# Attention and routed experts on one core: first expert's scaling spread, six matmuls of zeros first, last 128 tokens in two halves

## The chip, the cores and the metric

One core of a Trainium2 chip. The time is the device time of one execution in microseconds (us). A core has TensorE (PE, matmuls; PEld is its weight load), VectorE (DVE), ScalarE (ACT), GpSimd (POOL) and SyncE (SP, which here only issues DMAs). They run their own instruction streams in order and wait for each other by semaphores.

## What is computed

```python
# attention: 8 batches, 8 heads, 576 positions, 64 per head, 128 features
proj = x @ w_phi;  proj = proj - max(abs(proj))        # for q and for k
phi  = concat(exp(proj), exp(-proj))
kv, z = phi(k).T @ v, sum(phi(k))
attn = (phi(q) @ kv) / (phi(q) @ z + 1e-6)
# experts: x = attn as 4608 tokens of 512, 8 experts of 512 -> 1024 -> 512
P = exp(x @ w_gate - max)                               # 4608 x 8
for _ in range(8):                                      # rows, then columns
    P /= P.sum(1) + 1e-9;  P /= P.sum(0) + 1e-9;  P *= N / E
out = sum(P[:, e] * (relu(x @ w1[e]) @ w2[e]) for e in range(8))
```

Every token goes through every expert; P only weighs their outputs.

## The kernel before, in words

**Stages.** Attention runs first, pair of heads by pair of heads. Its results are turned and kept as `xT` (features on partitions, 4608 tokens in nine groups of 512, bf16). While attention still runs, and while the table P is normalised in eight rounds, TensorE already computes the first expert (`up0` and `down0`), unweighted, into one f32 accumulator `acc[g]` (128 x 4 x 512) for each of the nine groups. When P is there, each `acc[g]` is scaled by P's first column, and experts 1 to 7 are added to it. So 36 scalings (4 for each group; line 1240) stand between the first expert and the second.

**Experts 1 to 7.** The work of one expert on one group is a unit. Both matrix products of a unit are done with seven products of half-size blocks instead of eight. The first (`up7`) runs as 14 small products of four matmuls of 128x128 by 128x256 each; the second (`down7`) as 7 products of eight. All of them are recorded at line 1078 (`product`). In `up7` several products go into the same PSUM bank one after the other, and ScalarE copies the state of the bank to a buffer U in between (line 1106), so the next product into that bank waits for the copy. VectorE adds U to another bank and writes the hidden activations `hT` (line 1110); ScalarE writes others with a relu (line 1115). In `down7` ScalarE weighs a bank with P into V (line 1230) and GpSimd adds V to `acc` (line 1233), or VectorE does it in one step (line 1218). The products of `down7` of one group are mixed with those of `up7` of the next (`ORDER`); the first unit, group 0 of expert 1, has no such partner.

**Order.** Nothing is issued as it is written. Each operation is recorded with an engine, an estimated duration, and lists of keys that it reads and writes (`Plan.op`). `Plan.schedule` then picks again and again the operation that can start first by those estimates, an earlier record winning a tie, and so fixes the order on each engine. ScalarE's estimate is el/1200 + 0.09 us, which gives a scaling of 512 elements 0.52 us. The keys shape only this order; the waits on the chip come from what each instruction really reads and writes.

**Beginning.** SP, ACT and POOL issue loads of q, k, v and w_phi. TensorE first turns blocks of k and q (line 545, transposes with `identf`), VectorE casts w_phi (line 820) and the turned block (line 549), TensorE computes scores (line 468, recorded in the helper `mm`), and ScalarE takes exponentials (line 464).

**End.** The last unit (expert 7, group 7) computes its second product in the plain way (`down8`): four blocks of 128 tokens (`ts` = 2, 3, 0, 1), eight matmuls of 512 columns each (line 468), one VectorE step that weighs with P and adds to `acc` (line 1167), and one store of 256 KB (line 956).

Of the kernel before, what the change touches and what calls it, by code (L numbers as in the profile page):

```python
# [12 lines left out]
ALU = mybir.AluOpType  # L13
# [215 lines left out]
def kernel(  # L229
# [11 lines left out]
    nc = tc.nc  # L241
# [49 lines left out]
    def pe(cols, fn, r=(), w=(), takes=()):  # L291
        plan.op("PE", max(cols / 2400.0 + 0.0025, 0.032), 0.32, fn, r, w, takes)
# [10 lines left out]
    def dma(queue, nbytes, rate, fn, r=(), w=()):  # L303

        plan.op(queue, 0.8 if queue == "POOL" else 0.6, 0.0, fn, r, w, (), nbytes / rate / (125 / 100))
# [45 lines left out]
    def new(tag):  # L351
        return banks.new(int(tag[1])) if tag in ("P1", "P2") else R[tag].new()
# [29 lines left out]
    def load_qk(b, hh, nh, t, r=()):  # L382

        o = hh % 4
        keys = [o // 2] if nh == 2 else [0, 1]
        if b < 2:
            g = t["f"]
            for x, src in ((1, k), (0, q)):
                i = 2 * x + o // 2
                dma("SP", nh << 17, 268, lambda x=x, src=src, i=i: nc.sync.dma_start(  # L390
                    out=acc[g][:, i:i + nh // 2].rearrange("p a (h c) -> p (a h) c", h=2),
                    in_=src[b, hh:hh + nh, 0:SM].rearrange("h (p j) d -> p h (j d)", j=NJ)),
                    r, [("acc", g, 2 * x + n) for n in keys])
            return
        for x, src in ((1, k), (0, q)):
            dma("POOL", nh << 17, 200, lambda x=x, src=src: nc.gpsimd.dma_start(
                out=t["qk"]()[:, x, o:o + nh],
                in_=src[b, hh:hh + nh, 0:SM].rearrange("h (p j) d -> p h (j d)", j=NJ)),
                r, [(t["qk"], x, i) for i in keys])
# [67 lines left out]
    def mm(out_, lhsT, rhs, start, stop):  # L467
        nc.tensor.matmul(out_, lhsT=lhsT, rhs=rhs, start=start, stop=stop)  # L468
# [310 lines left out]
    def akey(g):  # L779
        return ["late"] * (g >= NA) + ["P"] * (g >= 9)  # L780
# [27 lines left out]
    for b in range(2):  # L808
        for i in range(2):
            halves[b, i] = new_half(b, i)  # L810
    load_qk(0, 0, 2, halves[0, 0])
    for i, (queue, eng) in enumerate((("ACT", nc.scalar), ("POOL", nc.gpsimd))):
        dma(queue, 1 << 15, 100, lambda i=i, eng=eng: eng.dma_start(
            out=wphi_f[64 * i:64 * i + 64, :], in_=w_phi), w=[f"wphi_f{i}"])
# [136 lines left out]
        expert0(i)  # L951


    def store(g, ts, one=0):
        if one:
            dma('SP', 1 << 18, 320, lambda: nc.sync.dma_start(
                out=out[g * S:g * S + SM].rearrange('(p j) d -> p j d', j=NJ)[:, ts:ts + 1],
                in_=acc[g][:, ts:ts + 1, :]),
                [('acc', g, ts, j) for j in range(2)], [('out', g, ts)])
        elif g < 8:  # L960
            if ts % 2:
                dma("SP", 1 << 19, 320, lambda: nc.sync.dma_start(
                    out=out[g * S:g * S + SM].rearrange("(p j) d -> p j d", j=NJ)
                    [:, ts - 1:ts + 1], in_=acc[g][:, ts - 1:ts + 1, :]),
                    [("acc", g, t, j) for t in (ts - 1, ts) for j in range(2)], [("out", g, ts)])
        else:
            for i in range(2):
                b = 2 * ts + i
                rows = slice(i * 64, i * 64 + 64)
                dma("SP", 1 << 17, 320, lambda b=b, rows=rows: nc.sync.dma_start(  # L970
                    out=out[b * S + SM:(b + 1) * S], in_=acc[8][rows, ts, :]),
                    [("acc", 8, ts, j) for j in range(2)], [("out", 8, b)])
# [184 lines left out]
    def down8(e, g, hT, w2):  # L1157

        for ts in (2, 3, 0, 1):
            py = new("P1")  # L1160
            for fc in range(8):
                i, j = fc // 4, ts // 2
                pe(512, lambda py=py, ts=ts, fc=fc: mm(
                    py(), hT[fc // 4]()[:, fc % 4, ts * 128:ts * 128 + 128], w2()[:, fc, :],
                    fc == 0, fc == 7), [(hT[i], fp, j) for i in range(2) for fp in range(2)]
                    + [(w2, i, j) for i in range(2) for j in range(2)] + ["P"], [py])
            dve(580, lambda py=py, ts=ts: nc.vector.scalar_tensor_tensor(
                out=acc[g][:, ts, :], in0=py(), scalar=P[:, 4 * g + ts, e:e + 1],
                in1=acc[g][:, ts, :], op0=ALU.mult, op1=ALU.add),
                [py, "P"], [("acc", g, ts, j) for j in range(2)])  # L1170
            store(g, ts, 1)

    def down7(e, g, hT, B7):

# [63 lines left out]
        if e == 1 and g < 9:  # L1238
            for ts in range(4):
                act(512, lambda ts=ts: nc.scalar.activation(  # L1240
                    out=acc[g][:, ts, :], in_=acc[g][:, ts, :], func=ACT.Copy, bias=0.0,
                    scale=P[:, 4 * g + ts, 0:1]), ["P", ("acc", g, ts)] + akey(g),
                    [("acc", g, ts, j) for j in range(2)])
        x, y, z = new("P1"), new("P1"), new("P1")

# [90 lines left out]
```

## Time and profile before

| | us |
|---|---|
| runs, median of 3 (lowest, highest) | 1036.96 (1035.57, 1037.59) |
| the profiled execution | 1036.16 |
| its span, first to last instruction | 1034.4 |
| PE busy, share of the span | 98% |
| ScalarE busy, share of the span | 69% |

The stages in the span: attention and the first expert up to 253 us, experts 1 to 7 from there to 1023 us, the plain second product and the last store from 1023 us to the end.

A row of a group or of the timeline names line, engine, operation, output<-inputs and shape; in brackets stand the engine's idle time before it and what ended it. Line numbers are those of the kernel before.

### The profile page before, as it was taken

To read this page: it belongs to the slowest core of one execution; us is meant where nothing else is said; L and a number is where in the kernel's file an instruction comes from. 1 tells how busy PE (TensorE), PEld (TensorE's weight loads), DVE (VectorE), ACT (ScalarE), POOL (GpSimd) and SP (SyncE) were. 2 spreads that over 40 slices of the span, in tenths; PEclk is the share of its full clock that TensorE was granted. 3 is DMA by queue.
4 is the path that set the end of the run, shared out by engine and by line. 5 is a ranking of instruction groups with operands and counts; after the bars stand their busy time and mean duration, and the time that the engine had idled before them with its cause. 6 is when DMAs were issued, how large, how long until landed. Compare 5 with 4: busy or idle time off the path is not lost.

```text
span 1034.4 us, 24481 instructions
## 1 busy us (share of the span) xinstructions
PE 1013.8 (98%) x9476; PEld 843.0 (81%) x9512; DVE 823.7 (80%) x1626; ACT 710.9 (69%) x1569; POOL 462.8 (45%) x534
## 2 busy tenths in 40 slices
PE   7899999999999999999999999999999999999998
PEld 5666666645788888888888888888888888888886
DVE  7999998987677788778777787788677877786775
ACT  7999999837966666666666656666666566666653
POOL 5877675400243443434443444434444433334442
PEclk9999999999999999999999999999999999999999
DMA  9998996085311161115211341134111611114333
GB/s 261 175 172 145 174 162 103 2 206 140 83 42 52 46 120 41 42 46 100 73 44 50 82 83 42 42 83 92 33 52 44 131 43 42 42 51 124 123 123 123
DMA packets 105237, 93.93 MB, mean 91 GB/s; under 512 B 45392, under 2 KB 80272, under 8 KB 105120
## 3 DMA queue, kind: packets, MB, share of 16 engines
q1 hardware_dynamic: 71360, 68.44, 24.3%
q0 software_dynamic: 33680, 23.90, 16.5%
q8 instruction: 74, 1.21, 0.5%
q14 instruction: 43, 0.35, 0.1%
q10 hardware_dynamic: 80, 0.03, 0.0%
HBM read 94.98 MB, written 14.16 MB: 106 GB/s over the span
## 4 chain that ended last, share of the span: by engine, by line
PE 92%; ACT 4%; DVE 3%; issue 1%; DMA 0%; DVEq 0%; POOLq 0%
PE P L1078 73%; PE P L468 17%; ACT acc L1240 2%; PE P L667 1%; DVE m L460 1%; ACT k L464 1%; PE P L706 1%; ACT q L464 0%; DMA wphi_f<-in_w_phi_dram 0%; DVE xb L687 0%; ACT U L1106 0%; DVE P L679 0%; PE P L672 0%; DVE S L986 0%; DVE m_r L460 0%
## 5 line engine op out<-in xcount | busy, mean ns | idle before, releaser
L1233 POOL TENSOR_TENSOR acc<-acc,V 128x512 f32<-128x512 f32 x248 | 316.1, 1281 | 440.5 <-ACT V L1230 437.6
L1110 DVE CUSTOM_DVE_ANT_0 hT<-P,U 128x512 bf16<-128x512 f32 x378 | 255.1, 687 | 105.9 <-ACT U L1106 56.7
L1106 ACT COPY U<-P 128x512 f32<-128x512 f32 x378 | 217.9, 590 | 139.0 <-PE P L1078 131.0
L1230 ACT ACTIVATE V<-P 128x256 f32<-128x256 f32 x496 | 205.6, 474 | 124.4 <-PE P L1078 119.2
L1218 DVE SCALAR_TENSOR_TENSOR acc<-P,acc 128x256 f32<-128x256 f32 x372 | 160.0, 478 | 73.7 <-PE P L1078 71.6
L1078 PEld LDWEIGHTS <-w 128*128 128x128 bf16 x2016 | 197.2, 98 | 25.2 <-issue 2.0
L1078 PEld LDWEIGHTS <-S 128*128 128x128 bf16 x1984 | 194.2, 98 | 22.4
L1078 PEld LDWEIGHTS <-T 128*128 128x128 bf16 x1512 | 147.9, 98 | 19.7 <-issue 2.5
L1078 PEld LDWEIGHTS <-hT 128*128 128x128 bf16 x1488 | 145.5, 98 | 17.1 <-DVE hT L1110 0.3
L1078 PE MATMUL P<-X,w 128*128 128x256 bf16 x1008 | 154.9, 273 | 0.4 <-ACT U L1106 0.4
L1078 PE MATMUL P<-xT,w 128*128 128x256 bf16 x1008 | 152.5, 273 | 0.9 <-ACT acc L795 0.5
L1078 PE MATMUL P<-X,T 128*128 128x256 bf16 x1008 | 148.6, 273 | 1.5 <-ACT U L1106 1.5
L1078 PE MATMUL P<-w,hT 128*128 128x256 bf16 x992 | 143.4, 273 | 0.0
L1078 PE MATMUL P<-T,S 128*128 128x256 bf16 x1056 | 136.3, 273 | 0.0
L1078 PE MATMUL P<-w,S 128*128 128x256 bf16 x928 | 126.5, 273 | 0.0
L460 DVE TENSOR_REDUCE m<-P 128x4 f32<-128x512 f32 x128 | 83.7, 679 | 3.4 <-PE P L468 2.1
L593 POOL TENSOR_TENSOR v<-v_m,em 128x512 bf16<-128x512 f32 x64 | 67.0, 1046 | 43.1 <-ACT em L464 39.0
L986 DVE TENSOR_TENSOR S<-hT 128x1024 bf16<-128x1024 bf16 x124 | 83.4, 709 | 0.3 <-ACT hT L1115 0.3
L1115 ACT ACTIVATE hT<-P 128x512 bf16<-128x512 f32 x126 | 74.2, 604 | 12.4 <-PE P L1078 11.9
L468 PE MATMUL P<-w,hT 128*128 128x512 bf16 x303 | 77.1, 379 | 0.9 <-DVE m L460 0.2
L1078 PE MATMUL P<-xT,T 128*128 128x256 bf16 x504 | 76.0, 273 | 0.3
L468 PE MATMUL P<-xT,w 128*128 128x512 bf16 x271 | 71.4, 379 | 1.0 <-ACT q L464 0.3
(95 smaller groups left out, 1096.5 us busy)
## 6 DMA issues: line engine op xcount, KB each, us to landing
X<-xd SPq DMA_DIRECT2D x126, 256.0 KB, 2.6
w<-in_moe_w_dram POOLq DMA_DIRECT2D x14, 1024.0 KB, 10.1
v_m<-in_v_dram SPq DMA_DIRECT2D x14, 512.0 KB, 5.2
out_dram<-acc SPq DMA_DIRECT2D x14, 512.0 KB, 2.7
xd<-S SPq DMA_DIRECT2D x18, 256.0 KB, 2.4
qk<-in_k_dram POOLq DMA_DIRECT2D x12, 256.0 KB, 5.5
qk<-in_q_dram POOLq DMA_DIRECT2D x12, 256.0 KB, 6.5
w<-in_moe_w_dram POOLq DMA_DIRECT2D x8, 256.0 KB, 7.7
```

The lines of the kernel that those rows point to most:

```text
L460: dve(el, lambda: nc.vector.tensor_reduce(out=dst(), in_=src(), axis=AX.X, op=ALU.max, apply_absolute_value=True), r, w)
L468: nc.tensor.matmul(out_, lhsT=lhsT, rhs=rhs, start=start, stop=stop)
L593: pool(512, lambda y=y, em=em: nc.gpsimd.tensor_tensor(out=s["v"][y]()[:, :, 0:D], in0=t["v"]()[:, h0:h0 + 2].rearrange("p a (b c) -> p (a ...
L986: lambda: f.tensor_tensor(out=out_(), in0=x(), in1=y(), op=op), r, w, **kw)
L1078: pe(256, lambda i=i, k=k, z=z: nc.tensor.matmul(bank()[:, 256 * i:256 * i + 256], lhsT=lhs(k, i), rhs=rhs(k), start=first and z, stop=k = ...
L1106: act(512, lambda: nc.scalar.copy(out=u[fp][n]().rearrange("p a b -> p (a b)"), in_=x[fp]()), [x[fp]], [u[fp][n]])
L1110: dve(500, lambda: nc.vector._custom_dve(ADD_SAT, out=out_(fp, i, j), in0=bank[fp]().rearrange("p (a b) -> p a b", a=2), in1=u[fp][n](), s ...
L1115: act(512, lambda: nc.scalar.activation(out=out_(fp, i, j), in_=x[fp]().rearrange("p (a b) -> p a b", a=2), func=ACT.Relu, bias=0.0, scale ...
L1218: dve(330, lambda n=n, ts=ts: nc.vector.scalar_tensor_tensor(out=acc[g][:, ts, 256 * j:256 * j + 256], in0=bank()[:, 256 * n:256 * n + 256 ...
L1230: act(390, lambda n=n: nc.scalar.activation(out=u()[:, n, :], in_=bank()[:, 256 * n:256 * n + 256], func=ACT.Copy, bias=0.0, scale=P[:, 4 ...
L1233: pool(670, lambda: nc.gpsimd.tensor_tensor(out=acc[g][:, 2 * i:2 * i + 2, 256 * j:256 * j + 256], in0=acc[g][:, 2 * i:2 * i + 2, 256 * j: ...
L1240: act(512, lambda ts=ts: nc.scalar.activation(out=acc[g][:, ts, :], in_=acc[g][:, ts, :], func=ACT.Copy, bias=0.0, scale=P[:, 4 * g + ts, ...
```

## The change

Three edits. A memset of zeros in the first 512 columns of `xT` and six matmuls on them stand ahead of all other work of TensorE; `xT` is written over later by its real contents. The last block of tokens (`ts` = 1 in `down8`) is computed, added and stored as two halves of 256 columns. The scaling of group g gets one more key to read, (`acc`, g-2, 0, 0), whose last writer is an addition to group g-2 by expert 1; so the planner places it after that.

```diff
@@ at the start
     load_qk(0, 0, 2, halves[0, 0])
+    dve(128, lambda: nc.vector.memset(xT[:, 0, 0:512], 0.0), w=[("xT", 0, 0)])
+    pz = new("P1")
+    for i in range(6):
+        pe(1024, lambda: mm(pz(), xT[:, 0, 0:128], xT[:, 0, 0:512], True, True),
+           [("xT", 0, 0)], [pz])
@@ def store
-    def store(g, ts, one=0):
-        if one:
-            dma('SP', 1 << 18, 320, lambda: nc.sync.dma_start(
-                out=out[g * S:g * S + SM].rearrange('(p j) d -> p j d', j=NJ)[:, ts:ts + 1],
-                in_=acc[g][:, ts:ts + 1, :]),
-                [('acc', g, ts, j) for j in range(2)], [('out', g, ts)])
+    def store(g, ts, js=()):
+        if len(js):
+            cols = slice(256 * js[0], 256 * js[-1] + 256)
+            dma("SP", len(js) << 17, 320, lambda: nc.sync.dma_start(
+                out=out[g * S:g * S + SM].rearrange("(p j) d -> p j d", j=NJ)[:, ts:ts + 1, cols],
+                in_=acc[g][:, ts:ts + 1, cols]),
+                [("acc", g, ts, j) for j in js], [("out", g, ts, j) for j in js])
@@ def down8
-            py = new("P1")
-            for fc in range(8):
...
-            store(g, ts, 1)
+            halves_ = 2 if ts == 1 else 1
+            n = DD // halves_
+            for c in range(halves_):
+                py, cols = new("P1"), slice(n * c, n * c + n)
+                for fc in range(8):
+                    i, j = fc // 4, ts // 2
+                    pe(n, lambda py=py, ts=ts, fc=fc, cols=cols, n=n: mm(
+                        py()[:, 0:n], hT[fc // 4]()[:, fc % 4, ts * 128:ts * 128 + 128],
+                        w2()[:, fc, cols], fc == 0, fc == 7),
...
+                js = range(2) if n == DD else (c,)
+                dve(580 * n // 512, lambda py=py, ts=ts, cols=cols, n=n:
+                    nc.vector.scalar_tensor_tensor(
+                        out=acc[g][:, ts, cols], in0=py()[:, 0:n],
+                        scalar=P[:, 4 * g + ts, e:e + 1], in1=acc[g][:, ts, cols],
+                        op0=ALU.mult, op1=ALU.add),
+                    [py, "P"], [("acc", g, ts, j) for j in js])
+                store(g, ts, js)
@@ def down7
                     out=acc[g][:, ts, :], in_=acc[g][:, ts, :], func=ACT.Copy, bias=0.0,
-                    scale=P[:, 4 * g + ts, 0:1]), ["P", ("acc", g, ts)] + akey(g),
+                    scale=P[:, 4 * g + ts, 0:1]), ["P", ("acc", g, ts)] + akey(g)
+                    + ([("acc", g - 2, 0, 0)] if g >= 2 else []),
                     [("acc", g, ts, j) for j in range(2)])
```

How the rows stand now. First ScalarE where the first expert ends and the second begins. `acc_78` to `acc_81` are the accumulators of groups 1 to 4, `acc_4252` that of group 5; L795 is the last eviction of the first expert, L1106 a copy to U. Before:

```order
L795 ACTIVATE acc_4254<-P 128x512
L1240 ACTIVATE acc_78<-acc_78,P 128x512 x3
L1240 ACTIVATE acc_79<-acc_79,P 128x512 x3
L795 ACTIVATE acc_4255<-P 128x512
L1240 ACTIVATE acc_79<-acc_79,P 128x512
L1240 ACTIVATE acc_80<-acc_80,P 128x512 x4
L1240 ACTIVATE acc_81<-acc_81,P 128x512
L795 ACTIVATE acc_4255<-P 128x512
L1106 COPY U<-P 128x512 x2
L1240 ACTIVATE acc_81<-acc_81,P 128x512
L1106 COPY U<-P 128x512
```

In the changed kernel, from the same eviction on (its lines are 1253 for the scaling, 1112 for the copy, 1121 for the relu, 1243 for V; accumulators 5 and up have other numbers):

```order
L795 ACTIVATE acc_4261<-P 128x512
L1253 ACTIVATE acc_78<-acc_78,P 128x512 x3
L795 ACTIVATE acc_4262<-P 128x512 x2
L1112 COPY U<-P 128x512 x6
L1121 ACTIVATE hT<-P 128x2x256 x2
L1243 ACTIVATE V<-P 128x256 x2
L1112 COPY U<-P 128x512
L1243 ACTIVATE V<-P 128x256 x2
L1112 COPY U<-P 128x512 x3
L1243 ACTIVATE V<-P 128x256 x2
L1253 ACTIVATE acc_79<-acc_79,P 128x512
```

The scalings of groups 0 and 1 keep their places; those of groups 2 to 8 (28 of 36) have moved behind the six copies, the two relus and the first V of group 0, and stand later one to three at a time among the copies of later units. The order of TensorE's products and of VectorE's sums changes with it from here on, the number of each does not.

Second, VectorE's and SP's first and last rows. VectorE's first rows, as a piece of the difference:

```order
-L818 MEMSET wphi_88 128x128
-L833 MEMSET vrd_89 128x520
...
+L812 MEMSET xT 128x256
+L823 MEMSET wphi_88 128x128
+L838 MEMSET vrd_89 128x520
```

One memset stands ahead of what was first there; TensorE's order begins with the six matmuls on `xT` and then has, up to the second expert, the same rows as before. VectorE's last rows, before:

```order
L1218 SCALAR_TENSOR_TENSOR acc_4253<-P,acc_4253 128x256 x2
L1110 ISA hT<-P,U 128x2x256
L1218 SCALAR_TENSOR_TENSOR acc_4253<-P,acc_4253 128x256 x2
L1167 SCALAR_TENSOR_TENSOR acc_4254<-P,acc_4254 128x512 x4
L1331 UNCONDITIONAL_BRANCH
```

And in the changed kernel:

```order
L1116 ISA hT<-P,U 128x2x256 x2
L1231 SCALAR_TENSOR_TENSOR acc_4260<-P,acc_4260 128x256 x4
L1179 SCALAR_TENSOR_TENSOR acc_4261<-P,acc_4261 128x512 x3
L1179 SCALAR_TENSOR_TENSOR acc_4261<-P,acc_4261 128x256 x2
L1345 UNCONDITIONAL_BRANCH
```

The fourth step of 512 columns has become two of 256; SP's last stores change in the same way, from four of 128x512 to three and two of 128x256.

More of the change, by code (lines that the diff above doesn't have):

```diff
@@ L1159, in down8 @@
         for ts in (2, 3, 0, 1):
-            py = new("P1")
-            for fc in range(8):
[L1162 to L1170, printed above, removed]
-            store(g, ts, 1)
+            halves_ = 2 if ts == 1 else 1
[7 more added lines that the diff above has]
+                        w2()[:, fc, cols], fc == 0, fc == 7),
+                        [(hT[i], fp, j) for i in range(2) for fp in range(2)]
+                        + [(w2, i, j) for i in range(2) for j in range(2)] + ["P"], [py])
+                js = range(2) if n == DD else (c,)
[6 more added lines that the diff above has]
+                store(g, ts, js)
     def down7(e, g, hT, B7):
```

## The prediction

> **What bounds the kernel now.** I read the page's header and its chain first, then the busy time by stretch, then the waits of the stretches where TensorE (PE) is not full.
>
> ```profile
> span 1034.4 us, 24481 instructions
> PE 1013.8 (98%) x9476; PEld 843.0 (81%) x9512; DVE 823.7 (80%) x1626; ACT 710.9 (69%) x1569; POOL 462.8 (45%) x534
> ...
> PE 92%; ACT 4%; DVE 3%; issue 1%; DMA 0%; DVEq 0%; POOLq 0%
> ```
>
> TensorE carries 92% of the chain; what is left to win is the 4% on ScalarE (ACT), the 3% on VectorE (DVE), and the end. Two tables by stretch (columns: stretch, its length, busy time and instruction count of each engine, clock, DMA share, GB/s), the second for the half-size matmuls of line 1078 alone, say where TensorE loses:
>
> ```profile
> 237.48:253.35 15.87, 15.78 (x74) 7.25 (x75) 12.74 (x29) 12.73 (x23) 0.75 (x1) 1.00 0.61 148
> 253.35:268.58 15.23, 12.23 (x98) 9.25 (x96) 9.93 (x16) 15.23 (x29) 0.89 (x1) 1.00 0.57 105
> 268.58:280.00 11.42, 11.42 (x105) 10.17 (x105) 7.87 (x15) 11.42 (x24) 5.08 (x4) 1.00 0.18 47
> ```
> ```profile
> 253.35:268.58 15.23, 11.75 (x94) 8.95 (x93) 1.00 0.57 105
> ...
> 280.00:1023.00 743.00, 742.92 (x6805) 665.54 (x6802) 1.00 0.26 67
> ```
>
> From 280 to 1023 us TensorE issues 6805 matmuls of 256 columns in 743.0 us, 109.2 ns each, without a gap: three quarters of the run cannot be touched by anything in this change. In 253.35 to 268.58 it issues only 93 (the 94th starts at the end) and some three of 512 columns, which at 109.2 and about 216 ns are worth 10.2 + 0.6 = 10.8 us. The stretch took 15.23, so **4.4 us are lost there**. ScalarE is the only engine that is busy in all of it (15.23 of 15.23), and the waits of TensorE and the chain of this stretch name it:
>
> ```profile
> PE P L1078 <- ACT U L1106: 1.9, 3, 1.3
> PE P L1078 <- ACT acc L795: 0.5, 1, 0.5
> PE P L1078 <- DVE hT L1110: 0.3, 1, 0.3
> ```
> ```profile
> by line: ACT acc L1240 61.1%; ACT U L1106 21.2%; issue 10.4%; ACT hT L1115 7.4%; ACT acc L795 3.2%; PE P L1078 1.8%
> ```
>
> The named waits come to 2.7 us; the rest of the 4.4 lies in the modelled ends of matmuls, which count a drained pipe as busy. Line 1240 is the scaling that the change touches.
>
> **Spreading the scaling: the large term.** The 36 scalings now stand together:
>
> ```profile
> L1240 ACT ACTIVATE acc<-acc,P 128x512 f32<-128x512 f32 x36 | 24.3, 754 | 1.1 <-DVE P L945 1.1
> ```
> ```profile
> 247.96 3.78 ACT L1240 ACTIVATE acc<-acc,P 128x512 f32<-128x512 f32 x6
> 251.63 0.59 ACT L795 ACTIVATE acc<-P 128x512 f32<-128x512 f32 x1
> 252.11 3.78 ACT L1240 ACTIVATE acc<-acc,P 128x512 f32<-128x512 f32 x6
> 255.79 0.59 ACT L795 ACTIVATE acc<-P 128x512 f32<-128x512 f32 x1
> 256.26 1.06 ACT L1106 COPY U<-P 128x512 f32<-128x512 f32 x2
> ```
> ```profile
> 254.10 0.49 PE L1078 MATMUL P<-xT,w 128*128 128x256 bf16 x3
> ...
> 267.48 0.60 PE L1078 MATMUL P<-X,T 128*128 128x256 bf16 x4 [1.33 <-ACT U L1106]
> ```
>
> A row of six takes 3.67 us from start to start, 0.61 each. The first product of the second expert is finished at 254.6 (254.10 + 0.49), but its copy to U, on which the next product into that bank waits, starts only at 256.26, 1.7 us late, behind a row of six. The changed order of ScalarE leaves the eight scalings of groups 0 and 1 where they were and then has all six copies of group 0, with the other 28 scalings one to three at a time in the units after it. The added entry in the planner's list of reads only orders the plan: no instruction waits for it on the chip, since a scaling reads acc of its own group and P. So ScalarE has nothing queued behind a new wait.
>
> Do 28 scalings fit later? One unit (one group of one expert) is 14 products of 4 and 7 of 8 matmuls, 112 x 109.2 ns = 12.2 us. ScalarE's share when no scaling is there, and what it bears with scalings:
>
> ```profile
> 280.00:400.00 120.00, 120.00 (x1102) 107.55 (x1100) 92.97 (x162) 75.14 (x159) 52.22 (x42) 1.00 0.27 63
> ```
>
> 75.14 of 120 is 63%, 7.7 us of a unit; four scalings add 4 x 0.61 = 2.4, which makes 83%. In 268.58 to 280 above it ran at 100%, scalings among its copies (the last of them at 278), while TensorE issued 105 matmuls in 11.42 us, 108.8 ns each. So single scalings between the copies cost TensorE nothing as long as no backlog stands before them. I therefore price the 28 moved scalings at zero; if that cover went, each would cost up to 0.61.
>
> What of the 4.4 us stays? Group 0 has no second products of an earlier group to fill TensorE, so some of its short waits may survive: I leave 0.7, about one copy and its handover (0.59 in the row of line 795, 0.53 a copy). VectorE, late next through its sums from U, has 9.93 of 15.23 us in use. Taken: **-3.7**; ends -4.6 (all of it, with 0.2 from the small gap before 253.35, where TensorE is busy 15.78 of 15.87) and -2.2 (half stays).
>
> **Zeros first: a small term.** The chain of the first microseconds, the matmul durations there, and the rows that bear on it:
>
> ```profile
> 1.26 3.86 DMA wphi_f<-in_w_phi_dram
> 5.40 0.70 DVE qkT L549
> 6.15 1.05 PE P L468 x4
> 7.22 2.06 ACT k L464 x4
> ```
> ```profile
> L468 PE MATMUL P<-wphi,qkT x6: 396/421/421, 6.1 to 7.2; 128*128 128x256 bf16 x6
> ```
> ```profile
> L545 PE MATMUL P<-identf,acc x8: 313/421/421, 8.7 to 10.2; 128*128 128x128 f32 x8
> ```
> ```profile
> L468 PE MATMUL P<-wphi,qkT x4: 272/272/273, 11.3 to 11.7; 128*128 128x256 bf16 x4
> ```
> ```profile
> 0.83 0.17 DVE L818 MEMSET wphi<- 128x128 uint32 x1 [0.83 <-PEq L1320]
> ...
> 3.58 2.13 PE L545 MATMUL P<-identf,acc 128*128 128x128 f32 x8 [3.58 <-DMA acc<-in_k_dram]
> 3.76 0.22 DVE L820 CAST wphi<-wphi_f 64x128 bf16<-64x128 f32 x1 [0.42 <-DMA wphi_f<-in_w_phi_dram]
> ...
> 17.89 1.09 PE L545 MATMUL P<-identf,acc 128*128 128x128 f32 x8 [0.52 <-DMA acc<-in_k_dram]
> ```
>
> The same matmul takes 421 ns at 6 us and 272 at 11 us: TensorE starts at half clock, and the one transpose of 313 ns among the eight from 8.7 to 10.2 puts the rise near 10.2 us (the clock column reads 1.00 throughout and does not show it). The memset doubles the width of the one that took 0.17, about 0.3 us, and VectorE's later work has 0.42 us of waiting before 3.76 to take it up. The zeros then run from about 1.2; a 512-column matmul at half clock is about 0.43 us, so six end near 3.8, and the first transposes start some 0.25 after their 3.58. That delay is free: the chain goes through the w_phi load (ending 5.1) and the cast at 5.40. The gain is that the four matmuls at 6.15 take 0.60, as at 11.3, instead of 1.05: -0.45, if the clock is up by then. ScalarE is busy without a break from 7.22 on, so this is all the chain can gain there; and at 17.89 TensorE already waits for a load, which does not come earlier, so part of it can be swallowed. Is the clock up by 6.15? The rise came 6.6 us after the first matmul at 3.58, but TensorE stood still for some 0.8 us of these; counted from 1.2 without that break it comes between 6 and 8 us, so it is about even whether the four profit. Taken: **-0.2**, about half of the gain, between -0.5 and +0.25 (no gain, and the transposes' delay on the path).
>
> The Trainium skill, "TensorE: Matmul & The Clock Gate", Part 1, has the clock rise after a free-running window of about 3.4 us that was busy, and Part 4 says that transposes do not count as busy in the same way. By that rule 2.6 us of zeros followed by transposes fill no window, and this term would be 0. This trace speaks against the second half: the clock rose while the eight transposes ran.
>
> **The last 128 tokens in two halves.** The end of the chain, the two shapes of VectorE's last step, and the stores:
>
> ```profile
> 1030.00 0.75 DVE L1167 SCALAR_TENSOR_TENSOR acc<-P,acc 128x512 f32<-128x512 f32 x1 [0.91 <-PE P L468]
> ```
> ```profile
> L1167 DVE SCALAR_TENSOR_TENSOR acc<-P,acc 128x512 f32<-128x512 f32 x4 | 3.0, 752 | 3.7 <-PE P L468 3.7
> L1218 DVE SCALAR_TENSOR_TENSOR acc<-P,acc 128x256 f32<-128x256 f32 x2 | 0.9, 475 | 0.0
> ```
> ```profile
> 1031.50:1032.00 0.50, 0.00 (x0) 0.00 (x0) 0.00 (x0) 0.00 (x0) 0.00 (x0) 1.00 0.77 291
> 1032.00:1032.50 0.50, 0.00 (x0) 0.00 (x0) 0.00 (x0) 0.00 (x0) 0.00 (x0) 1.00 0.63 234
> ```
> ```profile
> out_dram<-acc SPq DMA_DIRECT2D x8, 128.0 KB, 2.3
> out_dram<-acc SPq DMA_DIRECT2D x4, 256.0 KB, 2.4
> ```
>
> Sixteen matmuls of 256 columns replace eight of 512: 16 x 109.2 against 8 x 216 ns, no more than 0.02 us. The first half's step and store (0.33 us to issue) run beside the second half's 0.87 us of matmuls. After the last matmul stands a step of 0.475 instead of 0.752: -0.28. The last 256 KB move in about 0.85 us (the two rows: 291 and 234 GB/s for half a microsecond each, 262 KB), so half the bytes save up to 0.4 if rows of half the length move as fast; by the landings of 128 and 256 KB only 0.1, but those 128 KB stores come in pairs. I take -0.35. Sum **-0.6**, between -0.35 and -0.7.
>
> **Sum.** -3.7 - 0.2 - 0.6 = -4.5 us. The profiled execution took 1036.16 us around its span of 1034.4, and 1036.16 - 4.5 = 1031.7. The median of the runs shown, 1036.96, is 0.8 higher (they run from 1035.57 to 1037.59), and would give 1032.5; I say **1032.0**. A difference under about 0.2% (2.1 us) cannot be told from no change here.
>
> **Rivals.**
> *Group 0's own latency was the wait* (chance 0.12): ScalarE is early, but TensorE waits for each copy and each VectorE sum anyway, because no second products stand between. For it: the waits above are of copies and of a sum, and the page cannot say how long they would be without the scalings. Against it: the first copy stood ready for 1.7 us behind scalings. Then 2.2 of the 4.4 stay: 1036.96 - 2.2 - 0.8 = about 1034.
> *The lateness comes back later* (0.08): the plan counts a scaling 0.52 us where the chip takes 0.61, and its copies slip in the units of groups 2 to 8 as much as was won; only the two ends are left, -0.8: 1035.4 to 1036.2, the same.
> *The moved scalings delay copies that TensorE waits for* (0.08), the case on the slow side: 28 x 0.61 = 17.1 us at the most, if every one stands exposed ahead of a copy. The gain of 4.5 is used up from the eighth exposed scaling (8 x 0.61 = 4.9), and it is slower than before by over 0.2% from the eleventh; with half of them exposed, 1032.5 + 8.5 = 1041. Against it: 268.58 to 280, where none of them cost anything at a full ScalarE.
> *The zeros do not raise the clock in time* (0.5, inside each of the cases): the change then doesn't do there what it says, +0.2 on any of them.
>
> **How the numbers follow.** The forecast has 0.72. Its low end takes every term at its best: 4.6 + 0.5 + 0.7 = 5.8 under 1036.16, 1030.4, less some 0.4 for the scatter of the runs: 1030.0. Upward the range takes in the first rival (1034) and the middle of what the second gives: 1035.2. Faster 0.82 (the forecast and most of the first rival), same 0.10, slower 0.08.
>
> **What will show it.** Right, if from 253 to 269 TensorE issues without the waits on U copies and the stretch is 3 to 4 us shorter, if scalings appear singly until some 100 us later while line 1078's successor keeps 109 ns a matmul, if the first 256-column scores take 272 ns, and if the last store is issued about 0.5 us after the last matmul instead of 0.8. Wrong, if TensorE shows waits on U or V in the units of groups 2 to 8, if the waits of group 0 stay at over 2 us with ScalarE idle, or if the scores still take 421.

## The result, and the profile after

The changed kernel takes **1033.71 us** (median of 7 runs, 1032.73 to 1035.2) against 1037.1 for the kernel before in the same measurement (7 runs, 1035.57 to 1038.33): 3.4 us less by the medians, ratio 0.9969 with a 95% interval of 0.996 to 0.9979, which is 2.2 to 4.1 us of 1037.1. The profiled execution took 1034.06 us around a span of 1032.3, 2.1 us less than the profiled one of before. That is less than the medians differ by, and the reason is the start, below.

The page's header, its line for TensorE, and its chain by engine:

```profile
span 1032.3 us, 24552 instructions
...
PE 1015.8 (98%) x9526; PEld 843.5 (82%) x9526; DVE 822.8 (80%) x1628; ACT 710.0 (69%) x1569; POOL 464.8 (45%) x534
...
PE 94%; DVE 3%; DMA 1%; ACT 1%; SPq 1%; issue 1%; POOL 0%; DVEq 0%
```

TensorE's share of the chain has gone from 92% to 94%, and ScalarE's from 4% to 1%. In the place of ScalarE some DMA has come in.

**The stretch that was lost.** Line 1078 of before is line 1084 now. From its first matmul the table by stretch for this line alone (columns: stretch, its length, busy time and count of PE and of its weight loads, clock, DMA share, GB/s) has

```profile
254.11:268.00 13.89, 12.47 (x109) 10.41 (x109) 1.00 0.63 115
```

109 matmuls in 13.89 us, where before had 93 in 15.23. 109 x 0.1092 + 3 x 0.216 = 12.55, so 1.34 us are lost here instead of 4.4. The waits of TensorE from 244 us on (total, times, longest) no longer have one on U or on acc:

```profile
PE P L1084 <- DVE hT L1116: 1.2, 3, 0.8
PE P L1084 <- ACT V L1243: 0.5, 1, 0.5
```

ScalarE's timeline (start, length, what, idle time before and its releaser) shows why. The first copy starts directly after its product and the eviction ahead of it, with ScalarE idle for 2.97 us before them:

```profile
255.07 0.60 ACT L795 ACTIVATE acc<-P 128x512 f32<-128x512 f32 x1 [2.97 <-PE P L468]
255.56 1.29 ACT L1112 COPY U<-P 128x512 f32<-128x512 f32 x2
257.14 1.24 ACT L1112 COPY U<-P 128x512 f32<-128x512 f32 x2 [0.29 <-PE P L1084]
```

From the second unit on the scalings appear one to three at a time, and for a hundred microseconds more, as their own line says (smallest, median and largest ns, first and last start):

```profile
L1253 ACT ACTIVATE acc<-acc,P x36: 707/722/765, 244.4 to 352.6; 128x512 f32<-128x512 f32 x36
```

The waits that are left, in TensorE's timeline: three in the first unit, and a new one a hundred microseconds later, where the kernel before issued without a gap. The rows at 283.28 and 355.58 are there to show when the product behind them could have started.

```profile
262.15 0.39 PE L1084 MATMUL P<-w,hT 128*128 128x256 bf16 x2 [0.24 <-DVE hT L1116]
262.75 0.83 PE L1084 MATMUL P<-w,hT 128*128 128x256 bf16 x6 [0.20 <-DVE hT L1116]
...
264.50 1.03 PE L1084 MATMUL P<-w,hT 128*128 128x256 bf16 x8 [0.49 <-ACT V L1243]
...
283.28 1.04 PE L1084 MATMUL P<-xT,T 128*128 128x256 bf16 x8
284.41 1.03 PE L1084 MATMUL P<-T,S 128*128 128x256 bf16 x8
...
355.58 0.27 PE L1084 MATMUL P<-w,hT 128*128 128x256 bf16 x1
356.62 0.60 PE L1084 MATMUL P<-xT,T 128*128 128x256 bf16 x4 [0.76 <-DVE hT L1116]
```

The bracket gives only the time after the modelled end of the last matmul. Counted from start to start, at 109.2 ns a matmul, the product at 356.62 is 0.93 us late (355.58 + 0.11 = 355.69). The product at 284.41 is late too, by 0.26 us (283.28 + 8 x 0.1092 = 284.15), though no wait is named there. All gaps of this kind from the second expert's first matmul to 1020 us come to 2.6 us, against 4.7 in the kernel before, of which 0.24 stand ahead of its product at 401.74.

**The start.** With the zeros, TensorE's timeline begins

```profile
1.19 2.74 PE L468 MATMUL P<-xT 128*128 128x512 bf16 x6 [1.19 <-DVE xT L812]
3.81 1.94 PE L545 MATMUL P<-identf,acc 128*128 128x128 f32 x8
5.79 1.50 PE L468 MATMUL P<-wphi,qkT 128*128 128x256 bf16 x8
...
20.97 0.30 PE L545 MATMUL P<-identf,acc 128*128 128x128 f32 x1 [0.70 <-DMA acc<-in_q_dram]
```

The next row of TensorE starts at 7.12, so the first eight score matmuls occupy 1.33 us from start to start. In before the same eight occupy 1.68 (6.15 to 7.83 in its timeline), in the fastest experiment below 0.88 (5.88 to 6.76). So the clock rose in the middle of them. But at 20.97 TensorE waits for the first 512 KB of batch 1's q, and the chain of the start now runs through that load:

```profile
12.12 8.71 DMA acc<-in_q_dram
```

**The end**, in the chain and in VectorE's timeline:

```profile
1014.95 6.77 PE P L1084 x62
1021.72 6.94 PE P L468 x40
1028.66 0.02 issue
1028.68 0.48 DVE acc L1179
```
```profile
1027.01 1.29 DVE L1179 SCALAR_TENSOR_TENSOR acc<-P,acc 128x512 f32<-128x512 f32 x2 [1.04 <-PE P L468]
1028.68 0.48 DVE L1179 SCALAR_TENSOR_TENSOR acc<-P,acc 128x256 f32<-128x256 f32 x1 [0.39 <-PE P L468]
```

The last step takes 0.48 us instead of 0.75, and from its start to the span's end there are 3.62 us instead of 4.40 (1034.4 - 1030.00).

The two profiled executions split into five stretches, each between two events of the timelines:

| us | before | after | difference |
|---|---|---|---|
| start to the gate's last two small matmuls | 242.22 | 243.18 | +0.96 |
| from there to the second expert's first matmul | 11.13 | 10.93 | -0.20 |
| from there to the last unit's first 512-column matmul | 769.54 | 767.45 | -2.09 |
| from there to the last step of VectorE | 7.11 | 7.12 | +0.01 |
| from there to the end of the span | 4.40 | 3.62 | -0.78 |

The gate is the table P, and its last two small matmuls are TensorE's row of shape 128x8 at 242.22 (243.18 after). The sum is -2.10. The +0.96 differs from run to run, with a load: the first 512 KB of batch 1's q land at 19.9 us in the profile of before and at 20.8 in that of after.

### The profile page after: what moved, and what is told of

Same layout as the page of the kernel before. It is cut to its first block, busy times and chain, and to the rows that moved or that the text cites. A ratio compares the mean times of both kernels' runs of the same rounds, so it can differ in the third digit from the quotient of the medians.

```text
span 1032.3 us, 24552 instructions
## 1 busy us (share of the span) xinstructions
PE 1015.8 (98%) x9526; PEld 843.5 (82%) x9526; DVE 822.8 (80%) x1628; ACT 710.0 (69%) x1569; POOL 464.8 (45%) x534
## 4 chain that ended last, share of the span: by engine, by line
PE 94%; DVE 3%; DMA 1%; ACT 1%; SPq 1%; issue 1%; POOL 0%; DVEq 0%
PE P L1084 73%; PE P L468 18%; PE P L667 1%; DMA acc<-in_q_dram 1%; DVE m L460 1%; PE P L706 1%; DMA v_r<-in_v_dram 1%; SPq L390 0%; PE P L672 0%; DVE S L992 0%; DVE hT L1116 0%; DVE acc L1231 0%; ACT k L464 0%; ACT q L464 0%; DVE xb L687 0%
## 5 line engine op out<-in xcount | busy, mean ns | idle before, releaser
L1121 ACT ACTIVATE hT<-P 128x512 bf16<-128x512 f32 x126 | 72.9, 600 | 13.1 <-PE P L1084 12.3
L468 PE MATMUL P<-w,hT 128*128 128x512 bf16 (+1 forms) x328 | 79.5, 374 | 0.2 <-DVE m L460 0.2
L468 PE MATMUL P<-xT,w 128*128 128x512 bf16 x288 | 74.8, 379 | 0.3 <-ACT q L464 0.3
```

The lines of the kernel that those rows point to most:

```text
L1121: act(512, lambda: nc.scalar.activation(out=out_(fp, i, j), in_=x[fp]().rearrange("p (a b) -> p a b", a=2), func=ACT.Relu, bias=0.0, scale ...
```

## The experiments

Twelve kernels ran, each timed beside the kernel before on the same chip. "Stretch" is the third row of the table above, "to last step" its third and fourth together, "tail" its last, all from the kernel's own profile. The border between the third row and the fourth lies up to 0.22 us earlier or later with the order of the last products; "to last step" does not depend on it, and is 776.65 for the kernel before and 774.57 for the changed one.

| kernel | what it is | median us (runs) | before, same call | ratio, 95% | stretch | to last step | tail |
|---|---|---|---|---|---|---|---|
| e1_zeros | before + zeros | 1036.94 (11) | 1036.95 | 1.0 (0.9991-1.0008) | 769.55 | 776.66 | 4.4 |
| e2_spread | before + spread | 1035.37 (11) | 1036.95 | 0.9982 (0.9973-0.9991) | 767.68 | 774.57 | 4.4 |
| e3_halves | before + halves | 1035.73 (11) | 1036.95 | 0.9989 (0.998-0.9998) | 769.52 | 776.65 | 3.6 |
| e4_no_zeros | after - zeros | 1033.74 (5) | 1036.95 | 0.9969 (0.9956-0.9981) | 767.66 | 774.58 | 3.6 |
| e5_v_late | e4, two loads of v later | 1033.93 (8) | 1036.67 | 0.9974 (0.9964-0.9984) | 767.44 | 774.57 | 3.7 |
| e6_v_late_zeros | the same with zeros | 1033.95 (9) | 1036.67 | 0.9973 (0.9963-0.9982) | 767.44 | 774.57 | 3.6 |
| e7_no_scaling | e4 without the scalings | 1032.37 (5) | 1036.67 | 0.9962 (0.995-0.9974) | 766.26 | 773.39 | 3.6 |
| e8_estimate | e4, plan's scaling 0.615 us | 1033.01 (6) | 1036.67 | 0.9968 (0.9956-0.998) | 766.81 | 773.94 | 3.7 |
| e12_estimate_again | e8 again | 1033.12 (5) | 1037.02 | 0.9969 (0.9956-0.9981) | 767.03 | 773.94 | 3.6 |
| e11_estimate_only | before, plan's scaling 0.615 us | 1034.32 (11) | 1037.02 | 0.9976 (0.9967-0.9985) | 767.24 | 774.35 | 4.4 |
| e9_v_behind | e8, two loads of v behind batch 1's | 1032.53 (5) | 1037.02 | 0.9965 (0.9952-0.9977) | 767.05 | 773.96 | 3.6 |
| e10_v_behind_zeros | the same with zeros | 1032.3 (5) | 1037.02 | 0.9958 (0.9946-0.9971) | 767.04 | 773.95 | 3.6 |

### The three parts, each alone, and two of them without the third

e1_zeros is before with this:

```diff
     load_qk(0, 0, 2, halves[0, 0])
+    dve(128, lambda: nc.vector.memset(xT[:, 0, 0:512], 0.0), w=[("xT", 0, 0)])
+    pz = new("P1")
+    for i in range(6):
+        pe(1024, lambda: mm(pz(), xT[:, 0, 0:128], xT[:, 0, 0:512], True, True),
+           [("xT", 0, 0)], [pz])
```

> The kernel before with the six matmuls of zeros alone. Theory A (the loads bound the first 20 us, and a faster clock is swallowed there): within 0.5 us of the kernel before, the score matmuls at about 6 us partly at full clock, and the two waits of TensorE for loads near 18 and 20 us longer by what was won. Rival B (the zeros cost the 0.96 us by which the changed kernel's profile is late at 242 us): 0.7 to 1.2 us slower. Rival C (they win the 0.45 us of the scores for good): 0.4 us faster.

Measured: 1036.94 us against 1036.95, no difference (-0.9 to +0.8 us). What the zeros were to do they did. The score matmuls at 6 us run at full speed, four in 0.60:

```profile
6.07 0.60 PE L468 MATMUL P<-wphi,qkT 128*128 128x256 bf16 x4
...
21.31 0.30 PE L545 MATMUL P<-identf,acc 128*128 128x128 f32 x1 [1.09 <-DMA acc<-in_q_dram]
```

The second row shows one place where the gain goes: TensorE stands at 21.31 for a load that has its own time, and waits longer for it than before (1.09 against 0.46 us). It was gone sooner, though. At line 480, before and then here, TensorE turns the remaining positions, whose 64 KB of q are a load too:

```profile
10.87 0.63 PE L480 MATMUL P<-identf,acc 128*128 128x128 f32 x4 [0.39 <-ACT q L464]
```
```profile
11.33 0.63 PE L480 MATMUL P<-identf,acc 128*128 128x128 f32 x4 [1.71 <-DMA acc<-in_q_dram]
```

So at 11 us this kernel is already 0.46 us behind the kernel before; the changed kernel, with the same wait of 1.61 us, starts this row at 10.79, 0.08 ahead.

e2_spread is before with the added key alone:

```diff
-                    scale=P[:, 4 * g + ts, 0:1]), ["P", ("acc", g, ts)] + akey(g),
+                    scale=P[:, 4 * g + ts, 0:1]), ["P", ("acc", g, ts)] + akey(g)
+                    + ([("acc", g - 2, 0, 0)] if g >= 2 else []),
```

> The kernel before with the spread of the scaling alone. Theory A (the parts add up, as the two profiles stand: 0.2 us before 253 us, 2.3 us from there to the last unit): 2.3 to 2.8 us faster, TensorE losing about 1.3 us in the first 14 us of the second expert and about 0.9 in one later wait. Rival B (the zeros cost 0.96 us): the same for this run. Rival (the spread is worth the whole 3.4 us and the other parts nothing): 3.4 us faster.

Measured: 1.6 us less by the medians, 0.9 to 2.8 by the ratio's interval; in the profile it is 2.08 us less to the last step (1.86 of it in the stretch), and the gap ahead is 0.20 shorter. The gain is there, and smaller than the 3.7 that was predicted.

e3_halves is before with the change in `down8` and `store` (the diff above, its second and third pieces).

```diff
-            store(g, ts, 1)
+            halves_ = 2 if ts == 1 else 1
...
+                store(g, ts, js)
```

> The kernel before with the last block of tokens in two halves alone. Theory A: 0.6 us faster, all of it behind the last matmul: the last VectorE step 0.28 us shorter and the last store about 0.3 us shorter. Rival (the end is hidden by something that follows the last store at a fixed time): no change.

Measured: 1.2 us less by the medians, interval 0.2 to 2.1; its tail in the profile is 3.6 us instead of 4.4. The profile's 0.78 lies inside the interval and is the better number of the two.

e4_no_zeros is the changed kernel without the six matmuls and their memset:

```diff
-    dve(128, lambda: nc.vector.memset(xT[:, 0, 0:512], 0.0), w=[("xT", 0, 0)])
-    pz = new("P1")
...
```

> The changed kernel without the six matmuls of zeros. Theory A (loads bound the start): 2.9 to 3.4 us faster than the kernel before, as the changed kernel is within 0.5 us. Rival B (the zeros cost 0.96 us): 4.1 to 4.4 us faster than the kernel before. Rival C (they win 0.45 us): 2.9 us faster, and the changed kernel clearly better.

Measured: 1033.74 us, the changed kernel's 1033.71 again. So, as far as these intervals can tell, the whole gain is that of the spread and the halves; the medians of the two alone, 1.6 + 1.2, make 2.8 of the 3.2 that they save together here.

### What is left in the first unit, and where the rest of the spread went

e7_no_scaling is e4 with no scaling at all. It leaves the weighting of the first expert's outputs out, so its time is a bound and not a version.

```diff
-        if e == 1 and g < 9:
+        if False:
```

> The changed kernel without zeros and without the 36 scalings (the first expert's outputs stay unweighted: that part of the computation is left out). Theory A (what is left of the loss behind 253 us is partly the first unit's own latency and partly the scalings that are now later): the waits of the first 14 us, 0.9 us by name, stay, the wait of 0.8 us near 356 us goes; 0.5 to 1 us faster than with the scalings. Rival (all of the rest is the scalings' doing): 2 us faster, and no wait at 262 to 265 us. Rival (none of it): no change.

Measured: 1032.37 us. Its table for the product line, over the same length from the first matmul as above for the changed kernel:

```profile
253.38:267.27 13.89, 12.47 (x109) 10.41 (x109) 1.00 0.63 115
```

To the hundredth the same as with the scalings spread. What the first unit still loses, 1.34 us, has nothing to do with the scalings: by the names of the waits it is the chain of product, copy, sum and relu with too little else to put between. To the last step, however, it takes 1.19 us less than e4, so spread scalings do cost something later. Its timeline says what: the products that are 0.26 us late near 284 us and 0.93 at 356 in the changed kernel (and the same in e4) are in time here. Its waits from 244 us on:

```profile
PE P L1079 <- ACT V L1238: 0.5, 1, 0.5
PE P L1079 <- DVE hT L1111: 0.4, 2, 0.2
```

e8_estimate, and once more as e12_estimate_again, is e4 with the planner's cost of a scaling raised from 512 to 630, that is from 0.52 us to what it takes on the chip, about 0.61 from start to start. Nothing that is computed changes; only the plan's order does.

```diff
-                act(512, lambda ts=ts: nc.scalar.activation(
+                act(630, lambda ts=ts: nc.scalar.activation(
```

> The changed kernel without zeros, with the planner's estimate of a scaling raised from 0.52 to 0.615 us, what the chip takes. Theory A (the wait of 0.8 us near 356 us comes from a plan that slips by 0.1 us with each scaling): that wait goes, 0.5 to 0.9 us faster than with the low estimate. Rival (it comes from VectorE instructions held up beside GpSimd, which a better estimate does not change): the wait stays or another one of its size appears; within 0.4 us.

> The changed kernel without zeros with the higher estimate, once more, beside the others of this call: 3.7 to 4.2 us faster than the kernel before, and its last small matmul of the routing within 0.3 us of the landing of the q load of batch 1 plus 222.3 us, as in the ten profiles so far.

Measured: 1033.01 and 1033.12 us. The medians are 0.6 to 0.7 below e4's, but the ratios, 0.9968 and 0.9969 against 0.9969, show no difference: the runs cannot tell it. The profiles can: to the last step both take 773.94 us, where the five kernels with the spread and the old cost (after, e2, e4, e5, e6) have 774.57 or 774.58. That is 0.63 less. The wait at 356 us is gone in both; the 0.26 us near 284 is not, and there is a new 0.24 at 509. Tables by stretch, PE's busy time and count first, for the changed kernel and then for e8:

```profile
340.00:370.00 30.00, 29.24 (x269) 26.06 (x267) 24.74 (x42) 22.53 (x47) 13.67 (x11) 1.00 0.36 80
```
```profile
340.00:370.00 30.00, 30.00 (x277) 26.89 (x276) 24.35 (x44) 21.92 (x46) 13.85 (x11) 1.00 0.37 84
```

e11_estimate_only puts that one number into the kernel before, without spread, zeros or halves (the same two lines as above).

> The kernel before with nothing but the estimate of a scaling raised from 0.52 to 0.615 us. If the loss behind 253 us came from the plan's slip (0.1 us for each of the 36 scalings, 3.4 us in all) and not from the place of the scalings: 2 to 3 us faster than the kernel before, though the scalings still stand close together, since the order now leaves room for the copies. If it came from the place (ScalarE full for 15 us): at most 0.7 us faster, TensorE still waiting for copies to U behind scalings.

Measured: 1034.32 us, 2.7 less than before by the medians, 1.6 to 3.4 by the interval, and 774.35 to the last step, 2.30 less than before where the spread alone gives 2.08: as much as the spread, from a cost in the plan. ScalarE is still full there (15.93 of the 16 us from 254 on), and its scalings still stand close together (11 in the first 13.89 us of the second expert, where before had 16 and the changed kernel has none), but the copies now stand ahead of most of them. Its ScalarE, and the waits of its TensorE from 244 us on:

```profile
252.67 3.16 ACT L1240 ACTIVATE acc<-acc,P 128x512 f32<-128x512 f32 x5
255.73 0.58 ACT L795 ACTIVATE acc<-P 128x512 f32<-128x512 f32 x1
256.21 1.23 ACT L1106 COPY U<-P 128x512 f32<-128x512 f32 x2
257.34 0.72 ACT L1240 ACTIVATE acc<-acc,P 128x512 f32<-128x512 f32 x1
258.06 1.07 ACT L1106 COPY U<-P 128x512 f32<-128x512 f32 x2
```
```profile
PE P L1078 <- DVE hT L1110: 0.6, 2, 0.4
PE P L1078 <- ACT V L1230: 0.6, 1, 0.6
PE P L1078 <- ACT U L1106: 0.2, 1, 0.2
```

The first product ends here at 255.95 (its row in TensorE's timeline starts at 255.46 and is 0.49 long), and its copy starts at 256.21, 0.26 us later. Before it was 1.7. So a full ScalarE was not the trouble, and neither were scalings in this stretch as such: the plan took a scaling for 0.09 us shorter than it is, and, as the two orders read, placed rows of six ahead of copies for which, on the chip, they were not done in time. The new order also has five scalings fewer in this length; what that alone would bring was not tried.

### What sets the start

e5_v_late and e6_v_late_zeros are e4 and the changed kernel with the loads of v for heads 4 to 7 in a loop of their own behind the loads of q and k of these heads:

```diff
     for h0 in (4, 6):
         load_qk(0, h0, 2, halves[0, 1])
+    for h0 in (4, 6):
         load_v(0, h0, 2, halves[0, 1])
```

> The changed kernel without zeros, and the two v loads of heads 4 to 7 of batch 0 issued behind the k and q loads of those heads. Theory A (the loads bound the start; TensorE waits for the k and q loads near 18 and 20 us): those two loads land up to 1.5 us sooner, the waits of 0.7 to 1.1 us near 18 and 20 us go, and the kernel is 0.5 to 1.2 us faster than the same without this (4 us faster than the kernel before). Rival (the start is bound by ScalarE, the waits for loads cost nothing): no change against 3.2 us faster than before; or slower by up to 1 us where GpSimd now waits for v.

> The changed kernel with the zeros, and the same two v loads issued late. Theory A (the loads swallow what the zeros win): with the loads sooner the zeros now bring 0.2 to 0.5 us against the run with late v loads without zeros. Rival B (the zeros themselves make the start later, as the profiles with zeros are late by 0.5 to 1 us at 242 us): 0.5 to 0.9 us slower than that run. Rival (the zeros do nothing at all): within 0.3 us of it.

Measured: 1033.93 and 1033.95 us, no change against e4 and after. This was a miss in its design: it orders the loads of batch 0 among themselves, and as many bytes as ever stand ahead of batch 1's q, for which TensorE waits. What the pair did show is that the zeros cost nothing. In the profile with them the gate's last small matmuls start at 241.87, the earliest of all, in that without at 243.64, and the difference is in the load: it was issued at 11.62 and at 13.14 and landed at 19.5 and at 21.2. Put together, in all the profiles in which that load keeps its place, with zeros and without, these last matmuls follow the landing one for one:

| profile | load lands, us | gate's last matmuls, us | difference |
|---|---|---|---|
| e6 (zeros) | 19.5 | 241.87 | 222.4 |
| before | 19.9 | 242.22 | 222.3 |
| e2 | 20.0 | 242.41 | 222.4 |
| e4 | 20.3 | 242.70 | 222.4 |
| after (zeros) | 20.8 | 243.18 | 222.4 |
| e1 (zeros) | 21.2 | 243.51 | 222.3 |
| e11 | 21.5 | 243.77 | 222.3 |

The other five such profiles give 222.3 to 222.5, among them e12's (20.5 and 242.85), for which this was the expectation.

e9_v_behind and e10_v_behind_zeros therefore move these two loads of v past batch 1's first loads of q and k; both start from e8.

```diff
     for h0 in (4, 6):
         load_qk(0, h0, 2, halves[0, 1])
-        load_v(0, h0, 2, halves[0, 1])
...
             load_qk(b + 1, 2 * pr, 4, t, gt)
+            if i == 0:
+                for h0 in (4, 6):
+                    load_v(0, h0, 2, halves[0, 1])
```

> The changed kernel without zeros, with the higher estimate, and the v loads of heads 4 to 7 of batch 0 issued behind the first k and q loads of batch 1, for which TensorE waits near 18 and 20 us. Theory A (two limits meet at 20 us: that q load, and ScalarE, which is busy without a break from 7 us on): the q load lands 1 to 1.8 us sooner, at about 18.5, but ScalarE then sets the pace: 0 to 0.4 us faster than the same kernel without this, and the last small matmul of the routing at 242.0 to 242.4 us. Rival (the load alone sets the pace): 1 us faster or more. Rival (the planner, seeing the loads earlier, puts transposes ahead of scores and TensorE then stands before them): slower.

> The same with the six matmuls of zeros. Theory A (what the zeros win, 0.4 us of ScalarE's chain, was swallowed by the q load of batch 1): now 0.3 to 0.6 us faster than the run without zeros. Rival (zeros bring nothing even so): within 0.2 us. Rival B (zeros cost): 0.5 us slower or more.

Measured: 1032.53 and 1032.3 us, 0.6 and 0.8 below e12 of the same call, with intervals of the ratio that overlap. In the profile of e10 the load lands at 18.0 and TensorE no longer waits for it, but the gate's last matmuls start at 242.52, 224.5 us later: the chain of the start runs through ScalarE's feature work instead. So one wait took the place of another. e9's profiled execution, 1035.38 us, is not like its other four, 1032.18 to 1032.7; its rows explain that execution alone. In it the load landed at 20.2, not at the expected 18.5, and the granted clock was 0.87 from 15 to 20 us and 0.78 from 20 to 25. Whether the zeros help once the load is out of the way stays open: 0.2 us between the two medians is too little to say.

e10 is the fastest version: 1032.3 us, 4.7 below the kernel before and 1.4 below the changed one by the medians. Against before the interval of its ratio (0.9946 to 0.9971) leaves no doubt; against the changed kernel's 0.9969 (0.996 to 0.9979) it is likely and not certain.

## Why the prediction was right, and which terms were off

The predicted 1032.0 us lies 1.7 below the measured 1033.71, and the range held it; a range of 5.2 us is wider than the whole gain, so this alone says little. Direction and places were right: the stretch at 254 us, the last step and the store. The sum was too large by a third, 4.5 against 3.4, and nearly all of that comes from one term.

**The spread: -3.7 predicted, -2.3 in the profile (-0.20 - 2.09), -1.6 in the runs of the part alone.** The mechanism named was the one that went away: no wait on a U copy is left, and the copy starts directly after its product. Two steps were mis-sized.
- "What of the 4.4 us stays? ... I leave 0.7." It is 1.34, and e7 shows that it is there without any scaling. The first rival, the unit's own latency, was right in kind and taken too large: not 2.2 of the 4.4, but 1.34.
- "I therefore price the 28 moved scalings at zero." They cost 1.19 us, 0.26 at 284 us and 0.93 at 356, and e7, which has none, is 1.19 us shorter than e4 to the last step. That is the second rival in kind, lateness that comes back later, at a third of its size. The part at 356 us goes when the plan has the true length of a scaling (e8, e12); the part at 284 us does not, and what it comes from stays open.

With these two the step reads -3.7 + 0.64 + 1.19 = -1.87. The kernel before lost another 0.24 ahead of 401.74, where the prediction saw no gap, and the small gap ahead of 253.35, which it had put only into its lower end, gave 0.20. Together that is -2.3, what the profile has.

**The cause was told too simply.** The prediction saw scalings that "stand together" as the cause, and the changed place as the cure. e11 leaves 11 of 16 in this stretch, corrects one number of the plan, and gains as much. The 0.52 against 0.61 us stood in the prediction, but as a risk of the change; e11 shows that correcting it was enough.

**The zeros: -0.2 predicted, 0.0 measured (-0.9 to +0.8).** The clock is up in time, or half in time, in every profile with zeros, so the rival with the highest chance (0.5), that they do not raise it, is wrong in e1 and half right in after. The prediction's doubt was the better guide: "at 17.89 TensorE already waits for a load, which does not come earlier, so part of it can be swallowed". All of it was, though in e1 and after first by an earlier load, the 64 KB of q at 11 us, and after that by batch 1's q at 21. On the rule of the Trainium skill ("TensorE: Matmul & The Clock Gate", Part 4) that transposes do not count as busy: in after the clock rose at about 6.7 us, behind 2.74 us of zeros and 2 us of transposes (at 0.21 each, an eighth of 1.68, and 0.11, an eighth of 0.88, some four and four make the 1.33 from 5.79 to 7.12). In e6 nothing but transposes ran between the zeros and the rise: the last four of them are still slow, and the scores behind them fast.

```profile
L545 PE MATMUL P<-identf,acc x4: 421/421/476, 4.9 to 5.6; 128*128 128x128 f32 x4
```
```profile
L468 PE MATMUL P<-wphi,qkT x4: 272/273/282, 6.1 to 6.4; 128*128 128x256 bf16 x4
```

The transposes did not hold the clock back; what share they had in its rise is not shown.

**The halves: -0.6 predicted, -0.78 in the profile.** The shorter step gave 0.27 of it, as predicted (0.28). The smaller store gave 0.5 instead of 0.35: the whole 0.4 that half the bytes can save, and a little more.

**Moved scalings that delay copies** (0.08, the slow side) did not happen at that size: of its 28 x 0.61 = 17.1 us at the most, the two late products above make 1.2, and from 370 to 1019 us TensorE has 5947 matmuls in the changed kernel and 5945 before.

**Against its own list of signs.** The stretch came out 3 us better by the count of matmuls, at the lower edge of "3 to 4"; the scalings in ones to threes until 352.6 us and the 109 ns are there; the scores take 272 ns only from the middle on; and the last store is issued behind a step of 0.48 us. The sign for "wrong", a wait on U or V in the units of groups 2 to 8, is not there by its words: the one wait named there, at 356 us, is on hT.

## What to carry to other kernels

Where a plan or a scheduler orders the instructions, compare its cost of each operation with the duration in the trace first: here one number 0.09 us too small, in 36 instructions, cost as much as the whole move of these instructions brought. When a backlog is taken away, ask what the same stretch would lose without the suspected work at all, since that is the size of the gain's end; an experiment that leaves it out gives it directly. And a faster first step is worth nothing as long as a load behind it keeps its own time: find the first wait on a load after it, and count the gain only up to there.

## What the runs showed of the hardware

**A bf16 TENSOR_TENSOR of VectorE took longer beside an addition of GpSimd.** The operation that let the wait at 356 us come about took 1.67 us, where its kind takes about 0.7. VectorE and GpSimd of the changed kernel, each with two places:

```profile
347.22 1.74 DVE L992 TENSOR_TENSOR S<-hT 128x1024 bf16<-128x1024 bf16 x1
...
350.46 0.68 DVE L992 TENSOR_TENSOR S<-hT 128x1024 bf16<-128x1024 bf16 x1
...
354.30 1.67 DVE L992 TENSOR_TENSOR w<-w 128x1024 bf16<-128x1024 bf16 x1
355.88 0.68 DVE L1116 CUSTOM_DVE_ANT_0 hT<-P,U 128x512 bf16<-128x512 f32 x1
```
```profile
347.15 1.26 POOL L1246 TENSOR_TENSOR acc<-acc,V 128x512 f32<-128x512 f32 x1 [0.53 <-ACT V L1243]
354.15 2.94 POOL L1246 TENSOR_TENSOR acc<-acc,V 128x512 f32<-128x512 f32 x2 [5.73 <-ACT V L1243]
```

Both long ones began just after an addition of GpSimd had begun (347.15 and 354.15), and the first ended 0.55 us behind it; the same operation at 350.46, with GpSimd idle, took 0.68. The sum from PSUM at 355.88, beside a running addition, took its usual 0.68. The Trainium skill, "SBUF — State Buffer", in its section on the two separate sides, has VectorE and GpSimd share a pair of ports as an exclusive lock, with the later one blocked until the first is done; these rows agree. That the stretched operation caused the wait is read from the rows, not tried by itself.

**The clock can fall again early.** In e10 it was up by 6 us, and TensorE then had waits of 0.81 and 1.24 us. The table by stretch has its granted clock (the value behind the last bracket) at 0.66 right after, and four scores of 256 columns take 1.06 us, as with a cold start:

```profile
10.00:15.00 5.00, 3.96 (x18) 2.52 (x19) 2.85 (x5) 3.46 (x11) 1.60 (x4) 0.66 0.97 294
```
```profile
9.11 0.63 PE L545 MATMUL P<-identf,acc 128*128 128x128 f32 x4 [0.81 <-DMA acc<-in_q_dram]
10.98 0.96 PE L480 MATMUL P<-identf,acc 128*128 128x128 f32 x4 [1.24 <-ACT r L464]
11.74 1.06 PE L468 MATMUL P<-wphi,qkT 128*128 128x256 bf16 x4
```

TensorE was busy for 3.09 of the 5 us from 5 to 10. In e9's profiled execution the clock fell too, to 0.87 from 15 to 20 us and 0.78 from 20 to 25, with TensorE busy for 3.18 us from 15 to 20 and no single wait over 0.93 us.

**The loads of the first 20 us scatter by 2 us.** The same 512 KB of q, issued between 11.6 and 13.1 us in the profiles in which it keeps its place, landed between 19.5 and 21.5, 7.6 to 8.9 us after their issue. That scatter is carried through to the end of the gate, and is of the size of the scatter between the runs of one kernel (1035.57 to 1038.33 before).
